# Linear attention and GELU feed-forward on one core: PSUM banks by name, weight loads regrouped, chunk loads asked for later, and four stores further down SyncE's list

## The chip, the core and the metric

The kernel runs on one core of a Trainium2 chip. The metric is the time of one execution on the device in microseconds (us); the median of three runs is compared. A profile is one further execution, recorded by the hardware. Engines are named as the profile names them: PE (TensorE, with PEld for its weight loads), DVE (VectorE), ACT (ScalarE), POOL (GpSimd), SP (SyncE). Each has its own list of instructions and works it in order. Every load from device memory but the eight decay factors is issued from POOL's list, every store and every DMA transpose from SP's; all share the same 16 DMA engines.

## The reference

Attention with a decay per head, worked in blocks with a state carried along, and then a two-matrix feed-forward with exact GELU over the heads laid side by side:

```python
def _attn_ref(q, k, v, lam):                 # q, k, v: (4, 8, 768, 64)
    ...
    for b in range(nb):                      # blocks of 64 tokens
        intra = np.einsum('bhic,bhjc->bhij', qb, kb) * Dmask[None]
        intra = np.einsum('bhij,bhjd->bhid', intra, vb)
        inter = np.einsum('bhid,bhde->bhie', qb * lam_pow[None], kv_state)
        out[:, :, sl] = intra + inter
        kb_dec = kb * rev_pow[None]
        kv_state = lam_block * kv_state + np.einsum('bhsd,bhse->bhde', kb_dec, vb)

def _moe_ref(x, w_in, w_out):                # x: (3072, 512); w_in: (512, 2048); w_out: (2048, 512)
    h = x @ w_in
    g = 0.5 * h * (1.0 + erf(h * inv_sqrt2))
    return g @ w_out
```

## The kernel before

**Tiling.** The 768 tokens of each of the 4 batches are cut into 6 chunks of 128 tokens. Chunk `n` is batch `n % 4` of group `n // 4`, so there are 24 chunks in 6 groups. A group gives one `x` tile of 512 tokens (128 columns for each chunk), and the feed-forward `mlp(g)` runs over it: 16 blocks `m0` to `m15` of 4 matmuls each (the first matrix, one 128-wide slice of `d_ff` each, then a Gelu on ACT) and 16 parts `p0` to `p15` of 4 matmuls each (the second matrix). In group 0 the parts go over the four quarters of `w_out` one after the other: `p0` to `p3` need `o0-4`, `p4` to `p7` need `o4-8`, `p8` to `p11` need `o8-12`, `p12` to `p15` need `o12-16`. With `mlp(g, n2, n3)` the first `n3` slices begin before the group's last chunk is there: `a` and `b` blocks take the first two and the third chunk's columns of slices below `n2`, blocks from `n2` to `n3` take three chunks' columns, and the `l` blocks (`rest`) do the last chunk's columns of all of them.

**The order is written by hand.** The pool of tiles makes no order of its own; what the code issues first stands first in each engine's list. The dictionary that goes with `mlp(g)` names, for a block, what is issued ahead of it: `visit(f, d)` interleaves on PE the outputs of chunk `f` with the scores and state products of chunk `d`; `values(n)` makes `vd` (the values with their decay) and half of `k2` on POOL; `keys(n)` makes the other half on DVE; `request(n)` puts the two DMA transposes of chunk `n` (k and q into `kqT`) on SP's list; `fetch(...)` and `ask(...)` put loads on POOL's list; `store_held` puts group 0's output tiles, which were kept back, on SP's list.

**Names for the steps.** `ask("...")` at line 147 is the order of the first loads: `k3` and `q3` are chunk 3's keys and queries, `v2` the values of chunks 2 and 3, `i4-6` slices 4 and 5 of `w_in` (two DMAs, one for each half of the partitions), `o4-8` slices 4 to 7 of `w_out` (one DMA), `V1` the values of group 1 (four DMAs, line 106). Chunks 0 to 7 are transposed on PE (`transposed`, line 237, and `both_transposed`, lines 247 and 251), later chunks by DMA (lines 258 and 259). `keep_warm` (line 497) is matmuls on a zero tile while the first loads arrive. The PSUM banks are shared by tag: two for `mh`, two for `mo`, four for `at`, taken in rotation; a taker waits until the bank's last user is done.

POOL and SP wait, ahead of each DMA that they issue, for the eighth DMA before it in their own list (one semaphore for each of eight lanes); so no more than eight of POOL's loads are on their way at a time.

Of the kernel before, what the change touches and what calls it, by code (L numbers as in the profile page):

```python
# [15 lines left out]
def kernel(  # L16
# [10 lines left out]
    nc = tc.nc  # L27
# [21 lines left out]
    out_pool = ctx.enter_context(tc.tile_pool(name="outp", bufs=6))  # L49
    ps = ctx.enter_context(tc.tile_pool(name="ps", bufs=1, space=bass.MemoryType.PSUM))  # L50

    BANKS = dict(mh=2, mo=2, at=4)

    def bank(shape, dtype, tag, name):
        return ps.tile(shape, dtype, tag=tag, name=name, bufs=BANKS[tag])

# [87 lines left out]
            else:  # L144
                (load_w_in if name == "i" else load_w_out)(*(int(x) for x in at.split("-")))

    ask("k0 q0 k1 q1 v0 k2 q2 k3 q3 v2 i0-1 i1-2 i2-4 i4-6 i6-8 i8-12 i12-16 o0-4 k4 q4 o4-8 V1 o8-12 k5 o12-16 k6 q6")

    idle = consts.tile([128, 512], BF16)
    nc.vector.memset(idle, 0.0)  # L150
# [76 lines left out]

    def transposed(c, name, eng):

        if name == "k":  # L230
            c.t_ps = bank([128, 2, HP, C], BF16, "mh", "t_ps")
        t_ps = c.t_ps[:, "kq".index(name)]
        on = half("kq".index(name))
        for hp in range(HP):
            for j in range(2):
                for hi in range(2):
                    nc.tensor.transpose(t_ps[half(hi), hp, half(j)], c.kq[on, 2 * hp + hi, j, :], ident[on, on])
        if name == "k":
            dst, src = c.kT, t_ps
        else:  # L240
            dst, src = (t.rearrange(f"d hp ({o}) -> d hp p j", j=2) for t, o in ((c.qT, "p j"), (t_ps, "j p")))
        (nc.scalar.copy if eng is nc.scalar else eng.tensor_copy)(dst, src)
# [122 lines left out]
    def scores0(n, mask=True):  # L365
        c = live[n]
        c.sc = [bank([128, HP, C], F32, "at", f"sc{hi}_ps") for hi in range(2)]
        issue([[(c.sc[hi][:, hp, :], c.kT[half(hi), hp, :], c.qT[half(hi), hp, :], True) for hi in range(2)]
               for hp in range(HP)])
        if mask:  # L370
            mask0(n)
# [41 lines left out]
    def mlp(g, n2=0, n3=0):  # L413


        x_t = xT[g]
        g_t = g_pool.tile([128, NK2, T], BF16, tag="g", name="g_t")
        hs = {}

        def columns(kf, lo, up):  # L420
            for ki in range(NK1):
                nc.tensor.matmul(hs[kf][:, lo:up], w_in_t[:, ki, kf * 128:(kf + 1) * 128], x_t[:, ki, lo:up],  # L422
                                 start=(ki == 0 and lo == 0), stop=(ki == NK1 - 1), skip_group_check=True)

        def mm1(kf, lo, up, last):
            def run():
                if lo == 0:
                    hs[kf] = bank([128, T], F32, "mo" if kf < n2 else "mh", "h_ps")
                columns(kf, lo, up)
                if last:  # L430
                    nc.scalar.activation(g_t[:, kf, :up], hs[kf][:, :up], ACT.Gelu)  # L431
            return run

        def rest(kfs):
            def run():
                h_ps = bank([128, len(kfs), C], F32, "mh", "h_ps")
                for i, kf in enumerate(kfs):
                    for ki in range(NK1):
                        nc.tensor.matmul(h_ps[:, i, :], w_in_t[:, ki, kf * 128:(kf + 1) * 128], x_t[:, ki, T - C:],
                                         start=(i == 0 and ki == 0), stop=(ki == NK1 - 1), skip_group_check=True)  # L440
                nc.scalar.activation(g_t[:, kfs[0]:kfs[-1] + 1, T - C:], h_ps, ACT.Gelu)  # L441
            return run

        om = {}

        def store(io, ps_, w):
            n = w.stop - w.start
            o_sb = out_pool.tile([128, n], F32, tag=f"o_{n}", name="o_sb")
            r = io * S + g * C
            nc.scalar.copy(o_sb, ps_)  # L450
            if g == 0:
                held.append((r, w, o_sb))
            else:
                nc.sync.dma_start(out[r:r + C, w], o_sb)

        def mm2(io, part):
            def run():
                if part == 0:
                    om[io] = bank([128, d_model], F32, "mh" if g == 0 and io >= 2 else "mo", "o2_ps")
                for kf in range(part * 4, part * 4 + 4):  # L460
                    nc.tensor.matmul(om[io], g_t[:, kf, io * C:(io + 1) * C], w_out_t[:, kf, :],  # L461
                                     start=(kf == 0), stop=(kf == NK2 - 1))
                if part == NK2 // 4 - 1:
                    store(io, om[io], slice(0, d_model))
            return run

        def mm2_half(io, h):
            def run():
                w = slice(h * (d_model // 2), (h + 1) * (d_model // 2))
                o2 = bank([128, d_model // 2], F32, "mo", "o2_ps")  # L470
                for kf in range(NK2):
                    nc.tensor.matmul(o2, g_t[:, kf, io * C:(io + 1) * C], w_out_t[:, kf, w],  # L472
                                     start=(kf == 0), stop=(kf == NK2 - 1))
                store(io, o2, w)
            return run

        blocks = [(f"a{kf}", mm1(kf, 0, 2 * C, False)) for kf in range(n2)]
        blocks += [(f"b{kf}", mm1(kf, 2 * C, T - C, True)) for kf in range(n2)]
        blocks += [(f"m{kf}", mm1(kf, 0, T - C, True)) for kf in range(n2, n3)]
        blocks += [(f"l{i}", rest(list(range(i, min(i + 4, n3))))) for i in range(0, n3, 4)]  # L480
        blocks += [(f"m{kf}", mm1(kf, 0, T, True)) for kf in range(n3, NK2)]
        if g == 0:
# [9 lines left out]

    def keep_warm(n):
        if not idle_ps:
            idle_ps[0] = bank([128, 512], F32, "mo", "idle_ps")
        for _ in range(n):
            nc.tensor.matmul(idle_ps[0], idle[:, :128], idle, start=True, stop=True)  # L497

# [16 lines left out]
    keep_warm(3)  # L515
    scores0(0)
    transposed(live[1], "k", nc.scalar)
    keep_warm(1)
    transposed(live[1], "q", nc.scalar)
    make_lam_o()  # L520
    keep_warm(3)
# [1 line left out]
    keep_warm(2)  # L523
    outputs0(0)
    empty(live[0])
    keep_warm(2)
    outputs0(1)
    empty(live[1])
    transposed(live[2], "k", nc.scalar)
    keep_warm(1)  # L530
    transposed(live[2], "q", nc.scalar)
    keep_warm(1)
    transposed(live[3], "k", nc.scalar)
    keep_warm(1)
    scores0(2)
    transposed(live[3], "q", nc.scalar)
    make_lam()
    nc.scalar.activation(warm, pos, ACT.Gelu)
    keep_warm(4)
    scores0(3)  # L540
    keep_warm(3)
    outputs0(2)
    empty(live[2])
    keep_warm(2)


    alloc_x(1)
# [15 lines left out]
    def ahead_of_group_1():  # L563
# [10 lines left out]
        begin(8)  # L574
        begin(9)

    run_blocks(mlp(0, 2, 3), {
        "b0": [last_of_first],
        "m3": [ahead_of_group_1],
        "m6": [make_dmask] + [lambda n=n: decay_k0(n, nc.vector) for n in range(B)],  # L580
        "p0": [first_states, lambda: by_block(live[4], nc.vector, nc.vector)],
        "p2": [lambda: both_transposed(live[4])],
# [5 lines left out]
        "p14": [lambda: visit(5, 6), lambda: both_transposed(live[7]), lambda: request(8)],  # L588
    })
    visit(6, 7, first=True)  # L590
    store_held(slice(0, 2))

# [6 lines left out]
    def keys(n):  # L599
        by_block(live[n], None, nc.vector)  # L600
# [10 lines left out]
    def plan_of(g):  # L611
        if g == 1:
            n = 2 * B
            return {
                "a0": [lambda: values(n), lambda: request(n + 1)],
                "b0": [lambda: fetch(n + 2, n + 3)],
                "m4": [lambda: visit(n - 1, None)],
                "m5": [lambda: keys(n), lambda: store_held(slice(2, B)), lambda: request(n + 2, n + 3)],
                "l0": [lambda: values(n + 1)],
                "l4": [lambda: ask(f"k{n + 4} q{n + 4} k{n + 5} q{n + 5}")],  # L620
                "m7": [lambda: visit(None, n)],
                "m8": [lambda: values(n + 2), lambda: ask("V3"), lambda: begin(n + 4), lambda: begin(n + 5),
                       lambda: request(n + 4, n + 5)],
                "m9": [lambda: keys(n + 1)],
                "m12": [lambda: visit(n, n + 1)],
                "m13": [lambda: values(n + 3)],
                "m14": [lambda: keys(n + 2)],
                "p2": [lambda: visit(n + 1, n + 2)],
                "p3": [lambda: values(n + 4)],
                "p4": [lambda: keys(n + 3), lambda: fetch(n + 6, n + 7), lambda: request(n + 6, n + 7)],  # L630
                "p8": [lambda: visit(n + 2, n + 3)],
                "p10": [lambda: keys(n + 4)],
                "p14": [lambda: visit(n + 3, n + 4)],
            }
# [52 lines left out]
```

## Time and profile before

| what | value |
|---|---|
| median of 3 runs | 214.06 us (213.49 to 214.38) |
| the profiled execution, its own time | 214.3 us |
| its span | 212.5 us |
| granted TensorE clock | 1.00 |
| PE busy | 203.4 us (96% of the span), 2421 matmuls |
| DMA engines | nine tenths busy or more in nearly all slices of the first 143 us |
| loads (software queue) | 74624 packets, 13.64 MB |
| transposes and stores (hardware queue) | 21152 packets, 10.50 MB |

"Busy" on PE is counted from the start to the modelled end of each matmul, which overlap: a row that gives 379 ns for one matmul of 512 columns stands in a stream whose matmuls start some 216 ns apart (64 of them in 13.81 us in the last group). So PE's share hides nothing only where its stream is dense; its idle time in front of an instruction is in the waits, with what ended it. Waits are given as: who waited, for whom, us in total, how many times, the longest.

### The profile page before, as it was taken

Reading aid. Unit: us, or ns where it says so; the run is one execution under the profiler, and the core shown is the slowest. Engines: PE = TensorE matmul, PEld = TensorE weight load, DVE = VectorE, ACT = ScalarE, POOL = GpSimd, SP = SyncE. Lnnn points to the kernel's source line nnn. Section 1 sums busy time; section 2 is a strip of 40 time slices with the busy share of each in tenths; the row PEclk is TensorE's granted clock in tenths of the full one; section 3 lists DMA queues with packets and bytes.
Section 4 is the critical chain, followed back from the end, with each engine's and each line's share of the span. In section 5 each row is a group of like instructions: output and inputs, shape, how many; then the busy total and the mean of one; then the engine's idle time right before and its main releaser. Section 6 shows DMA issues by size and latency. Waiting matters only on the chain.

```text
span 212.5 us, 5590 instructions
## 1 busy us (share of the span) xinstructions
PE 203.4 (96%) x2421; PEld 101.9 (48%) x2421; DVE 86.2 (41%) x185; ACT 90.2 (42%) x165; POOL 104.8 (49%) x148
## 2 busy tenths in 40 slices
PE   7999999799999899999999999999999999999992
PEld 2456445355664354444444444444544444444461
DVE  4657904339555556728416624732330331000000
ACT  5557663039645411265412356321466211665120
POOL 8989555598999403999689950930000000000000
PEclk9999999999999999999999999999999999999999
DMA  6999999999999999999999999932100021100121
GB/s 59 147 164 140 195 191 178 194 141 131 121 188 217 122 153 112 87 152 236 144 101 105 151 266 122 133 102 99 51 3 0 3 82 66 52 0 0 52 87 62
DMA packets 95801, 24.49 MB, mean 115 GB/s; under 512 B 87968, under 2 KB 92832, under 8 KB 95776
## 3 DMA queue, kind: packets, MB, share of 16 engines
q0 software_dynamic: 74624, 13.64, 89.6%
q1 hardware_dynamic: 21152, 10.50, 27.4%
q8 instruction: 19, 0.31, 0.6%
q14 instruction: 6, 0.05, 0.1%
HBM read 27.27 MB, written 6.29 MB: 158 GB/s over the span
## 4 chain that ended last, share of the span: by engine, by line
PE 71%; DMA 16%; POOL 6%; ACT 3%; issue 1%; SPq 0%; POOLq 0%
PE o_ps L461 33%; PE h_ps L422 30%; DMA vg_t<-in_v_dram 5%; DMA kqT<-q_t 4%; DMA w_in_t<-in_moe_w_in_dram 3%; DMA kq_t<-in_q_dram 3%; PE sc_ps L346 3%; POOL kq_t L82 2%; PE o_ps L346 2%; POOL w_in_t L125 2%; PE o_ps L472 2%; PE kv_ps L346 2%; POOL vg_t L106 1%; POOL v_t L95 1%; ACT k L272 1%
## 5 line engine op out<-in xcount | busy, mean ns | idle before, releaser
L422 PE MATMUL h_ps<-x_t,w_in_t 128*128 128x512 bf16 (+3 forms) x400 | 84.2, 366 | 0.2 <-ACT g_t L441 0.2
L461 PE MATMUL o_ps<-w_out_t,g_t 128*128 128x512 bf16 x368 | 83.0, 379 | 0.0
L431 ACT ACTIVATE g_t<-h_ps 128x512 bf16<-128x512 f32 (+1 forms) x96 | 55.9, 587 | 32.4 <-PE h_ps L422 32.4
L422 PEld LDWEIGHTS <-w_in_t 128*128 128x128 bf16 x400 | 37.5, 98 | 41.2 <-issue 0.8
L461 PEld LDWEIGHTS <-g_t 128*128 128x128 bf16 x368 | 34.7, 98 | 40.3
L338 DVE TENSOR_TENSOR x_t<-o_ps,lam_o 128x512 bf16<-128x512 f32 x24 | 16.5, 689 | 67.2 <-PE o_ps L346 67.2
L450 ACT COPY o_sb<-o_ps 128x512 f32<-128x512 f32 (+1 forms) x25 | 14.2, 571 | 65.1 <-PE o_ps L461 62.6
L281 POOL TENSOR_TENSOR vd<-vg_t,lam_v 128x512 bf16<-128x512 bf16 x20 | 21.0, 1050 | 25.6 <-DMA vg_t<-in_v_dram 24.6
L71 POOL DMA_DIRECT2D k_t<-in_k_dram x20 | 18.1, 907 | 2.2 <-DMA w_out_t<-in_moe_w_out_dram 1.7
L292 DVE TENSOR_TENSOR sm<-sc_ps,dmask 128x512 bf16<-128x512 f32 x20 | 13.6, 682 | 10.3 <-PE sc_ps L346 10.2
L106 POOL DMA_DIRECT2D vg_t<-in_v_dram x20 | 16.5, 843 | 1.4 <-DMA w_in_t<-in_moe_w_in_dram 1.4
L268 POOL COPY k<-k_t 64x256 bf16<-64x256 bf16 x34 | 14.1, 414 | 1.0
L71 POOL DMA_DIRECT2D q_t<-in_q_dram x16 | 14.5, 907 | 0.0
L346 PEld LDWEIGHTS <-kqT 64*64 64x64 bf16 (+1 forms) x352 | 7.7, 107 | 11.8 <-issue 10.9
L497 PE MATMUL idle_ps<-idle 128*128 128x512 bf16 x33 | 11.1, 444 | 1.2 <-DVE idle L150 1.2
L346 PE MATMUL sc_ps<-kqT 64*64 64x64 bf16 (+1 forms) x352 | 10.4, 197 | 1.8 <-DMA kqT<-q_t 1.5
L272 DVE COPY k<-k_t 64x256 bf16<-64x256 bf16 x34 | 11.9, 350 | 0.5
L125 POOL DMA_DIRECT2D w_in_t<-in_moe_w_in_dram x14 | 8.7, 675 | 1.0 <-DMA kq_t<-in_q_dram 0.8
L346 PE MATMUL kv_ps<-vd,k 64*64 64x64 bf16 x288 | 8.0, 193 | 1.2 <-POOL vd L281 1.2
L317 DVE TENSOR_TENSOR state<-t,lam_c 128x256 bf16<-128x256 f32 x16 | 8.9, 558 | 0.5
L346 PE MATMUL o_ps<-sm,vg_t 64*64 64x64 bf16 x320 | 8.4, 193 | 0.0
L307 DVE TENSOR_TENSOR t<-kv_ps,state 128x256 f32<-128x256 f32 x16 | 6.6, 415 | 1.0 <-PE kv_ps L346 1.0
(73 smaller groups left out, 134.9 us busy)
## 6 DMA issues: line engine op xcount, KB each, us to landing
out_dram<-o_sb SPq DMA_DIRECT2D x23, 256.0 KB, 5.2
k_t<-in_k_dram POOLq DMA_DIRECT2D x20, 128.0 KB, 6.8
vg_t<-in_v_dram POOLq DMA_DIRECT2D x20, 128.0 KB, 10.9
w_out_t<-in_moe_w_out_dram POOLq DMA_DIRECT2D x4, 512.0 KB, 11.2
q_t<-in_q_dram POOLq DMA_DIRECT2D x16, 128.0 KB, 6.9
w_in_t<-in_moe_w_in_dram POOLq DMA_DIRECT2D x4, 256.0 KB, 7.7
w_in_t<-in_moe_w_in_dram POOLq DMA_DIRECT2D x6, 128.0 KB, 4.2
kq_t<-in_k_dram POOLq DMA_DIRECT2D x4, 128.0 KB, 4.6
```

The costliest lines, as they stand in the source:

```text
L71: nc.gpsimd.dma_start(t, dram[name][b, :, g * C:(g + 1) * C, :].rearrange("h si d -> si h d"))
L106: nc.gpsimd.dma_start(t[half(hi), u], src[hi, s:s + L])
L268: same.tensor_copy(c.k2[half(hi), hi], k_r[half(hi), :, hi, :])
L272: copy(c.k2[half(hi), 1 - hi], k_r[half(1 - hi), :, hi, :])
L281: nc.gpsimd.tensor_mul(vd[n], of_group(n), lam_vb)
L292: nc.vector.tensor_mul(c.sm, c.sc, dmask)
L338: nc.vector.tensor_mul(xT[c.g][:, :, c.b * C:(c.b + 1) * C], c.o, lam_o)
L346: nc.tensor.matmul(out_, lhsT, rhs, start=start, stop=True, skip_group_check=True)
L422: nc.tensor.matmul(hs[kf][:, lo:up], w_in_t[:, ki, kf * 128:(kf + 1) * 128], x_t[:, ki, lo:up], start=(ki == 0 and lo == 0), stop=(ki == N ...
L431: nc.scalar.activation(g_t[:, kf, :up], hs[kf][:, :up], ACT.Gelu)
L450: nc.scalar.copy(o_sb, ps_)
L461: nc.tensor.matmul(om[io], g_t[:, kf, io * C:(io + 1) * C], w_out_t[:, kf, :], start=(kf == 0), stop=(kf == NK2 - 1))
```

## The change

Five edits of order, one of the shape of loads; the arithmetic is the same.

1. PSUM tag `mo` (two banks in rotation) becomes `mo0` and `mo1` (one bank each, chosen by the slice or part number). The PE transposes of the first four chunks no longer put k and q in one bank: k's stay in `mh`, q's get `mo1`. `keep_warm` uses `mo0`.
2. The `keep_warm` matmuls before group 0 (33 in all, as before) and the transposes, scores and outputs of chunks 1 to 3 are put in another order.
3. `mlp(0, 2, 3)` becomes `mlp(0, 2, 2)`: slice 2 is done whole, after `l0`.
4. The first loads: `w_in` in 10 DMAs in place of 14, and `V1` ahead of `o4-8`; `o12-16` goes last.
5. In group 1 the loads of chunks 12 and 13 and of `V3` move from `l4` and `m8` to `m13`, with the transposes of 12 and 13.
6. Group 0's output tiles 0 and 1 go behind the transposes of chunk 9, tiles 2 and 3 behind those of chunk 11.

```diff
-    BANKS = dict(mh=2, mo=2, at=4)
+    BANKS = dict(mh=2, mo0=1, mo1=1, at=4)
...
-    ask("k0 q0 k1 q1 v0 k2 q2 k3 q3 v2 i0-1 i1-2 i2-4 i4-6 i6-8 i8-12 i12-16 o0-4 k4 q4 o4-8 V1 o8-12 k5 o12-16 k6 q6")
+    ask("k0 q0 k1 q1 v0 k2 q2 k3 q3 v2 i0-2 i2-4 i4-8 i8-12 i12-16 "
+        "o0-4 k4 q4 V1 o4-8 k5 o8-12 k6 q6 o12-16")
...
-        if name == "k":
-            c.t_ps = bank([128, 2, HP, C], BF16, "mh", "t_ps")
-        t_ps = c.t_ps[:, "kq".index(name)]
+        t_ps = bank([128, HP, C], BF16, "mh" if name == "k" else "mo1", "t_ps")
...
-                    hs[kf] = bank([128, T], F32, "mo" if kf < n2 else "mh", "h_ps")
+                    hs[kf] = bank([128, T], F32, f"mo{kf % 2}" if kf < n2 else "mh", "h_ps")
...
     transposed(live[1], "k", nc.scalar)
-    keep_warm(1)
+    keep_warm(2)
     transposed(live[1], "q", nc.scalar)
...
     outputs0(0)
     empty(live[0])
-    keep_warm(2)
+    keep_warm(1)
+    transposed(live[2], "k", nc.scalar)
     outputs0(1)
     empty(live[1])
-    transposed(live[2], "k", nc.scalar)
     keep_warm(1)
     transposed(live[2], "q", nc.scalar)
+    keep_warm(2)
+    transposed(live[3], "k", nc.scalar)
+    scores0(2)
     keep_warm(1)
-    transposed(live[3], "k", nc.scalar)
-    keep_warm(1)
-    scores0(2)
     transposed(live[3], "q", nc.scalar)
...
     scores0(3)
-    keep_warm(3)
+    keep_warm(1)
     outputs0(2)
     empty(live[2])
-    keep_warm(2)
+    keep_warm(3)
...
-    run_blocks(mlp(0, 2, 3), {
+    run_blocks(mlp(0, 2, 2), {
...
     visit(6, 7, first=True)
-    store_held(slice(0, 2))
...
-                "a0": [lambda: values(n), lambda: request(n + 1)],
+                "a0": [lambda: values(n), lambda: request(n + 1), lambda: store_held(slice(0, 2))],
...
-                "m5": [lambda: keys(n), lambda: store_held(slice(2, B)), lambda: request(n + 2, n + 3)],
+                "m5": [lambda: keys(n), lambda: request(n + 2, n + 3), lambda: store_held(slice(2, B))],
...
-                "l4": [lambda: ask(f"k{n + 4} q{n + 4} k{n + 5} q{n + 5}")],
...
-                "m8": [lambda: values(n + 2), lambda: ask("V3"), lambda: begin(n + 4), lambda: begin(n + 5),
-                       lambda: request(n + 4, n + 5)],
+                "m8": [lambda: values(n + 2)],
...
-                "m13": [lambda: values(n + 3)],
+                "m13": [lambda: values(n + 3), lambda: fetch(n + 4, n + 5), lambda: request(n + 4, n + 5)],
```

The other uses of `mo` become `mo0` or `mo1` in the same way (here `n` is 8, so `n + 4` is chunk 12). In the lists that result, POOL goes from `values(9)` to `values(10)` and `values(11)` and only then to the loads of chunks 12 and 13 and the four of `V3`; SP has the transposes of 8, of 9, two stores, the transposes of 10 and 11, two stores, the transposes of 12 and 13. PE has four matmuls fewer (slice 2's columns are no longer split).

More of the change, by code (lines that the diff above doesn't have):

```diff
@@ L458, in run @@
                 if part == 0:
-                    om[io] = bank([128, d_model], F32, "mh" if g == 0 and io >= 2 else "mo", "o2_ps")
+                    om[io] = bank([128, d_model], F32, "mh" if g == 0 and io >= 2 else f"mo{io % 2}", "o2_ps")
                 for kf in range(part * 4, part * 4 + 4):
@@ L469, in run @@
                 w = slice(h * (d_model // 2), (h + 1) * (d_model // 2))
-                o2 = bank([128, d_model // 2], F32, "mo", "o2_ps")
+                o2 = bank([128, d_model // 2], F32, f"mo{(io + h) % 2}", "o2_ps")
                 for kf in range(NK2):
@@ L494, in keep_warm @@
         if not idle_ps:
-            idle_ps[0] = bank([128, 512], F32, "mo", "idle_ps")
+            idle_ps[0] = bank([128, 512], F32, "mo0", "idle_ps")
         for _ in range(n):
@@ L575, in ahead_of_group_1 @@
         begin(9)
-    run_blocks(mlp(0, 2, 3), {
+    run_blocks(mlp(0, 2, 2), {
         "b0": [last_of_first],
-        "m3": [ahead_of_group_1],
+        "m2": [ahead_of_group_1],
         "m6": [make_dmask] + [lambda n=n: decay_k0(n, nc.vector) for n in range(B)],
```

## The prediction

> **What bounds the kernel now.** I read the waits of PE first, since PE is busy for 96% of the span. Columns: who waited, for whom, us in total, how many times, the longest.
>
> ```profile
> PE sc_ps L346 <- DMA kqT<-q_t: 1.5, 2, 1.1
> PE kv_ps L346 <- POOL vd L281: 1.2, 1, 1.2
> PE t_ps L237 <- ACT kqT L242: 0.7, 2, 0.4
> PE sc_ps L346 <- ACT kqT L254: 0.3, 1, 0.3
> PE h_ps L422 <- ACT g_t L441: 0.2, 1, 0.2
> ```
>
> These sum to 3.9 us. The PE timeline (start, us, what, idle before it) puts the three largest in place; behind 75.3 us there is none up to the end at 208.69.
>
> ```profile
> 40.71 0.44 PE L346 MATMUL kv_ps<-vd,k 64*64 64x64 bf16 x16 [1.24 <-POOL vd L281]
> ...
> 67.46 0.22 PE L346 MATMUL sc_ps<-kqT 64*64 64x64 bf16 x2 [0.36 <-DMA kqT<-q_t]
> ...
> 74.59 0.22 PE L346 MATMUL sc_ps<-kqT 64*64 64x64 bf16 x2 [1.14 <-DMA kqT<-q_t]
> ```
>
> So whatever PE gains by 75 us arrives whole at the end, unless a new wait takes it. Who is late for PE is read from POOL's timeline and the chain that ended last.
>
> ```profile
> 30.69 0.76 POOL L128 DMA_DIRECT2D w_out_t<-in_moe_w_out_dram  x1 [1.72 <-DMA w_out_t<-in_moe_w_out_dram]
> ...
> 35.55 0.89 POOL L71 DMA_DIRECT2D k_t<-in_k_dram  x1 [1.70 <-DMA w_out_t<-in_moe_w_out_dram]
> ...
> 39.61 1.04 POOL L281 TENSOR_TENSOR vd<-vg_t,lam_v 128x512 bf16<-128x512 bf16 x1 [2.26 <-DMA vg_t<-in_v_dram]
> ...
> 66.25 3.31 POOL L106 DMA_DIRECT2D vg_t<-in_v_dram  x4
> ...
> 82.95 1.04 POOL L281 TENSOR_TENSOR vd<-vg_t,lam_v 128x512 bf16<-128x512 bf16 x1 [11.43 <-DMA vg_t<-in_v_dram]
> ```
>
> ```profile
> 28.16 11.22 DMA vg_t<-in_v_dram
> ...
> 65.39 9.06 DMA kqT<-q_t
> ```
>
> The first loads are one saturated stream: each issue waits for the landing of the eighth before it (35.55: for o4-8, landed 35.26). V1 was issued by 28.97 and landed at 28.16 + 11.22 = 39.38. SP's own list is late in the same way, each issue taking over 1 us:
>
> ```profile
> 56.89 2.12 SPq L397 DMA_DIRECT2D out_dram<-o_sb  x2
> 59.11 1.29 SPq L258 DMA_TRANSPOSE kqT<-k_t  x1
> 60.45 1.85 SPq L259 DMA_TRANSPOSE kqT<-q_t  x1
> 62.34 1.15 SPq L397 DMA_DIRECT2D out_dram<-o_sb  x2
> 63.60 1.71 SPq L258 DMA_TRANSPOSE kqT<-k_t  x1
> 65.39 2.04 SPq L259 DMA_TRANSPOSE kqT<-q_t  x1
> ```
>
> **Edits 1 to 3, the start.** The two waits of 0.36 us of a q transpose for ACT (k and q in one bank) go. PE took up chunk 3's q at 14.59, though it had landed at 13.87; in the new order that is some 0.65 us earlier, and a0 (17.80) begins some 1 us earlier. Of that, l0 gives back about 0.3: without slice 2 ahead of it, it comes right behind the b blocks while DVE still empties chunk 3's outputs (0.69 us, L338). The four matmuls fewer save nothing (12 of 128 columns took 0.74 us, 62 ns each; 512 columns cost 216). So PE would reach p4 some 0.7 us ahead of the 37.2 of before. I count this as zero, because p4 then waits for o4-8 (next); if that cover is gone, it is worth 0.7.
>
> **Edit 4, the first loads.** The bytes stay, the packets change. By the trace's packet records, packets of 1024 bytes moved 200 KB/us (23 to 28 us), of 512 bytes 143 (16 to 20 us), of 256 bytes 157. i4-8 (512 KB as stored) goes from 512-byte to 1024-byte packets: 3.6 to 2.6 us, -1.0; i0-2 (256 KB) from 256 to 512 bytes: +0.16. The stream is then about 0.85 us ahead. V1 (4.12 us, landings 35.26 to 39.38) passes o4-8 (2.45 us, 32.81 to 35.26), so V1 lands at about 36.1 and its wait goes, but o4-8 lands last of the two, at 39.38 - 0.85 = 38.5, and p4 needs it: a new wait of some 2 us at p4. From there to p6 come p4 and p5 (8 matmuls at 217 ns, 1.73) and the scores and products of chunk 4 (0.65): p6 at 40.95 against 41.08. V1's 4.12 us contain a stall of the stream (a 16 KB instruction fetch at 37.08, 1.17 us in the packet records); if it falls behind o4-8 in the new order, p6 is at 40.3. I take a gain of 0.4 between the two; the bounds are +0.8, and -0.75 if the larger packets bring nothing (o4-8 at 39.38, p6 at 41.8). i4-8 as one pair may land at 21 to 22 us with m4 due at 21.0; up to 1 us, covered by the same wait at p4. Behind p6 the same 8.4 us of loads follow (39.38 to 47.77 before), and o8-12 and o12-16 land before p8 and p12 by some 0.5 to 1 us.
>
> A rule of the Trainium skill would make more of this edit: the page "DMA: Bandwidth & Descriptors", section "Anatomy of one DMA — SWDGE (gpsimd) path", gives each DMA a fixed 2.0 us beside its bytes, which for four DMAs fewer is, as an estimate, 8 us earlier. The rows speak against it: neighbouring w_in DMAs landed 0.3 to 1.3 us apart, though each took 3.6 to 8.7 us from issue to landing.
>
> **Edit 6, the stores.** k9 and q9 leave the two stores (2.12 us) behind, so q9 is issued 2.1 us earlier than 60.45; its wait was 0.36: gone. k10 and q10 have all four tiles' stores moved about them: stores 2 and 3 (1.15 us) go behind q11, stores 0 and 1 stay ahead of k10. PE will want q10 at 73.45 - 0.4 - 0.36 = 72.7 (73.45 is 74.59 less its wait); it landed at 74.45, so it must come 1.8 us earlier. 1.15 come from the stores, 0.85 from the stream ahead, and the loads of chunks 12 and 13 no longer share the engines with it (edit 5): with transposes beside them, loads and transposes moved 430 packets per us each, loads alone 1200. I take the 1.14 as gone; at worst it stays. The stores delay nobody: their tiles are next written in group 1's parts, from 77.2.
>
> **Edit 5, the later loads.** In POOL's list `values(10)` and `values(11)` now come first, and the copies of `values(11)` need k11 (landed at 62.81). So the four loads start at about 63.7 in place of 60.65, and V3 is issued from 67.3 to 70.6 in place of 66.25 to 69.56. Queued behind V3 is `values(12)`, and `visit(11, 12)` on PE waits for that. Before, V3 landed at 82.79, `values(12)` was done at 84.85, and PE came at 86.50: 1.65 us to spare. With 1.9 us gained PE comes at 84.6. V3's landing is bounded by 81.4 (the stream is 1.4 ahead: no wait) and 83.84 (1.05 later, as issued: done at 85.9, a wait of 1.3). As the stream stays full, I take 82.2 to 82.8: a wait of 0.3.
>
> Sum: 0.4 + 0.36 + 1.14 - 0.3 = 1.6 us. The profiled execution took 214.3 (span 212.5): 212.7. It stands 0.24 above the median of 214.06, so the predicted median is 212.5.
>
> **Rivals.**
>
> *V3 becomes the wait.* For it: PE arrives 1.9 us earlier with 1.65 to spare, and the issue moves back. Against it: between 60 and 83 us the engines, not POOL's issues, set the landings (13.2 us from V3's last issue to its landing). At 83.84 the gain is 0.4 + 1.5 - 1.3 = 0.6: 213.5. A chance of 0.17.
>
> *The transposes stay late.* For it: q10 took 9.06 us from issue to landing and q9 7.0; if their landing is set by engines that are full anyway, an earlier issue brings little. Then only 0.4 is left: 213.7. A chance of 0.12.
>
> *Slower: the loads of chunk 11 are held up by the transposes of chunk 9, and V3 with them.* Those transposes now run beside the loads of chunks 10 and 11 (430 packets per us in place of 1200). If k11 lands 2 us later (64.8), POOL, which stands at the copies of `values(11)`, issues all of V3 3 us later than before; at the same 13.2 us it lands at 85.8, `values(12)` is done at 87.8, and `visit(11, 12)` begins 1.3 us later than before: 215.4. It decides from a landing of V3 at 84.4 on (no gain at all), and 85.5 for 0.5%. Against it: the loads of chunk 8 to 11 should be asked for earlier. A chance of 0.12. The Trainium skill's page named above, in "Rules for kernel authors", advises to issue a DMA early and wait late; this edit does the opposite for eight loads, and no run here shows yet which side wins.
>
> *The fixed cost per DMA is real.* Then o4-8 and V1 both land before PE needs them, the wait of 1.24 and the start's 0.7 are won: 1.24 + 0.7 + 0.36 + 1.14 - 0.5 (V3) = 2.9: 211.1. A chance of 0.06.
>
> **Chances and range.** The forecast has 0.53, with its own range of 211.8 to 213.0; the rivals 0.47. A measurement of this kernel can tell about 0.5% (1.07 us) from no change. Faster by more than that is below 212.99: nearly all of the forecast (0.50), the last rival (0.06), some of the first two (0.07), 0.63. Slower than 215.1 has 0.13; within, 0.24. The range for 8 in 10 is 211.4 to 214.5: it takes in the first two rivals and leaves out most of the slower one and of the largest gain.
>
> **What would show it.** PE's waits should show a wait on `w_out_t` at p4 of 1 to 2.5 us in place of the 1.24 on `vd`; no wait on `kqT`; no `t_ps` wait on ACT; p6 near 40.7. `vd` of chunk 12 should start at 82 to 83, with a wait of `kv_ps` under 0.7 us near 84.6. It is wrong if o4-8 lands later than 39.4, if q10 lands after 73, or if `vd` of chunk 12 starts after 84.5.

## The result and the profile after

| | before | after |
|---|---|---|
| median, runs of both on one chip | 214.35 us (212.04 to 217.26, 20 runs) | 211.59 us (210.78 to 214.44, 20 runs) |
| ratio, 95% interval | | 0.9902 [0.9874, 0.9929] |
| the profiled execution, its own time | 214.3 us (span 212.5) | 212.24 us (span 210.4) |

The change is faster by about 1%, some 2.1 us, and the interval lies wholly below 0.995. The ratios leave out executions more than 1.5% slower than the fastest of their kernel, so they are not the quotients of the medians, and two of the profiles further down, those of `a_no_first` and `split_k`, were taken while the chip granted a clock of 0.992 in place of 1.00, so of these two only the ratio, and for `split_k` the loads before 30 us, are read.

The waits of PE in the changed kernel (who waited, for whom, us in total, how many times, the longest):

```profile
PE o_ps L460 <- issue: 1.6, 10, 0.2
...
PE kv_ps L345 <- issue: 1.1, 1, 1.1
...
PE h_ps L421 <- ACT g_t L440: 0.2, 1, 0.2
PE h_ps L438 <- DVE x_t L337: 0.2, 1, 0.2
PE t_ps L236 <- DMA kq_t<-in_q_dram: 0.2, 1, 0.2
```

The waits on `kqT`, on `vd` and on ACT's `kqT` are all gone, and no wait on `w_out_t` has come in their place. The ten short ones on `o_ps` are no waits: in the timeline they stand behind rows of three or seven matmuls where four or eight are issued, so a record is missing there. The largest new one is 1.1 us on `kv_ps` with no releaser ("issue": PE waited for nothing that the profile shows).

The row of before with which `p6` begins (start, us, what, idle before it):

```profile
41.08 2.76 PE L461 MATMUL o_ps<-w_out_t,g_t 128*128 128x512 bf16 x12
```

PE's timeline of the changed kernel shows where the time was won and lost:

```profile
38.92 0.44 PE L345 MATMUL sc_ps<-kqT 64*64 64x64 bf16 x16
39.20 0.42 PE L345 MATMUL kv_ps<-vd,k 64*64 64x64 bf16 x16
39.55 2.76 PE L460 MATMUL o_ps<-w_out_t,g_t 128*128 128x512 bf16 x11
...
50.46 0.22 PE L345 MATMUL kv_ps<-vd,k 64*64 64x64 bf16 x2 [1.12 <-issue]
...
72.45 0.22 PE L345 MATMUL sc_ps<-kqT 64*64 64x64 bf16 x2
```

`p6` begins at 39.55 in place of 41.08, so 1.53 us are won by there. 1.12 us are lost again in the middle of `visit(5, 6)`. Chunk 10's scores begin at 72.45 in place of 74.59, 2.14 earlier, and most of that difference stays to the end (PE's last matmul ends at 206.67 in place of 208.65, 1.98 earlier).

POOL's timeline answers to the rows of `vd` shown of before:

```profile
35.22 1.04 POOL L280 TENSOR_TENSOR vd<-vg_t,lam_v 128x512 bf16<-128x512 bf16 x1 [1.24 <-DMA vg_t<-in_v_dram]
...
83.05 1.04 POOL L280 TENSOR_TENSOR vd<-vg_t,lam_v 128x512 bf16<-128x512 bf16 x1 [13.01 <-DMA vg_t<-in_v_dram]
```

Chunk 4's `vd` starts at 35.22 (39.61 before). By their landing times the last of `w_in` is there at 25.99 (27.87 before), `V1` at 35.04 and `o4-8` at 36.92, both before PE comes to `p4` at about 37.1. Chunk 12's `vd` starts at 83.05 (82.95 before).

### The profile page after: what moved, and what is told of

The parts are those of the page before. It is cut to its first block, busy times and chain, and to the rows that moved or that the text cites. A ratio compares the mean times of both kernels' runs of the same rounds, so it can differ in the third digit from the quotient of the medians.

```text
span 210.4 us, 5549 instructions
## 1 busy us (share of the span) xinstructions
PE 200.5 (95%) x2388; PEld 101.1 (48%) x2417; DVE 81.7 (39%) x185; ACT 90.4 (43%) x165; POOL 102.0 (48%) x144
## 4 chain that ended last, share of the span: by engine, by line
PE 89%; POOL 3%; DMA 3%; issue 2%; ACT 0%; DVE 0%; POOLq 0%
PE h_ps L421 39%; PE o_ps L460 38%; PE sc_ps L345 3%; DMA kq_t<-in_q_dram 3%; PE o_ps L345 2%; POOL kq_t L82 2%; PE kv_ps L345 2%; PE o_ps L471 2%; PE idle_ps L496 1%; POOL v_t L95 1%; PE h_ps L438 1%; PE t_ps L250 1%; PE t_ps L246 0%; DVE x_t L337 0%; ACT g_t L440 0%
## 5 line engine op out<-in xcount | busy, mean ns | idle before, releaser
L460 PE MATMUL o_ps<-w_out_t,g_t 128*128 128x512 bf16 x354 | 80.5, 380 | 1.8 <-issue 1.6
L267 POOL COPY k<-k_t 64x256 bf16<-64x256 bf16 x34 | 13.6, 401 | 1.6 <-DMA k_t<-in_k_dram 0.6
L496 PE MATMUL idle_ps<-idle 128*128 128x512 bf16 x30 | 10.2, 449 | 1.5 <-DVE idle L151 1.2
L271 DVE COPY k<-k_t 64x256 bf16<-64x256 bf16 x34 | 10.7, 313 | 0.5
L316 DVE TENSOR_TENSOR state<-t,lam_c 128x256 bf16<-128x256 f32 x16 | 8.0, 499 | 0.5
L345 PEld LDWEIGHTS <-k 64*64 64x64 bf16 x288 | 6.5, 108 | 1.3 <-issue 1.2
```

The lines of the kernel that those rows point to most:

```text
L267: same.tensor_copy(c.k2[half(hi), hi], k_r[half(hi), :, hi, :])
L345: nc.tensor.matmul(out_, lhsT, rhs, start=start, stop=True, skip_group_check=True)
```

## The experiments

All ratios are to the kernel before, run beside each on the same chip. Several chips were used, so ratios are compared and not microseconds. The last three columns are read from one profile of each kernel: when the last load of `w_in` landed, when `p6` began and when chunk 10's scores began.

| kernel | edits in it | ratio [95%] | last `w_in` | p6 | chunk 10's scores |
|---|---|---|---|---|---|
| before | none | 1 | 27.87 | 41.08 | 74.59 |
| after | all | 0.9902 [0.9874, 0.9929] | 25.99 | 39.55 | 72.45 |
| first_loads | 4 | 0.9909 [0.9873, 0.9945] | 25.61 | 40.00 | 72.30 |
| regroup | grouping of `w_in` only | 0.9910 [0.9874, 0.9945] | 25.91 | 40.09 | 73.86 |
| stores | 6 | 0.9952 [0.9907, 0.9998] | 27.75 | 40.54 | 72.49 |
| start_only | 1 to 3 | 0.9953 [0.9907, 0.9999] | 28.31 | 41.48 | 74.93 |
| a_no_first | all but 4 | 0.9946 [0.9914, 0.9978] | | | |
| a_old_stores | all but 6 | 0.9905 [0.9870, 0.9941] | 26.12 | 39.55 | 71.55 |
| a_old_late | all but 5 | 0.9936 [0.9903, 0.9970] | 26.08 | 39.95 | 71.96 |
| split_k | grouping, in 14 DMAs | 0.9993 [0.9948, 1.0039] | 27.46 | | |
| no_56 | all but 5 and 6 | 0.9894 [0.9856, 0.9932] | 25.95 | 39.50 | 72.19 |
| after_again | all | 0.9875 [0.9839, 0.9911] | 25.66 | 39.58 | 72.10 |
| warm_small | all, and 99 matmuls more | 0.9893 [0.9855, 0.9930] | 25.10 | 39.90 | 72.04 |
| warm_half | all, and 33 matmuls more | 0.9901 [0.9863, 0.9938] | 25.89 | 41.24 | 73.24 |

### One edit alone

The first loads, edit 4 alone:

```diff
-    ask("k0 q0 k1 q1 v0 k2 q2 k3 q3 v2 i0-1 i1-2 i2-4 i4-6 i6-8 i8-12 i12-16 o0-4 k4 q4 o4-8 V1 o8-12 k5 o12-16 k6 q6")
+    ask("k0 q0 k1 q1 v0 k2 q2 k3 q3 v2 i0-2 i2-4 i4-8 i8-12 i12-16 "
+        "o0-4 k4 q4 V1 o4-8 k5 o8-12 k6 q6 o12-16")
```

> The kernel before with edit 4 alone (w_in in 10 DMAs, V1 ahead of o4-8, o12-16 last). Theory A (the larger w_in packets run the stream faster, whatever the start does): o4-8 lands at 37 to 37.5 us, V1 at 35 to 35.5, p6 starts at 39.6 to 40.0 (41.08 before), no wait for vd or w_out_t ahead of it; with the waits on kqT left in part, the time falls by 1 to 1.6 us (0.5 to 0.7%). Rival B (the earlier stream of the changed kernel comes from the new start, edits 1 to 3, or from an instruction fetch that fell better): o4-8 lands at 38 us or later as the prediction had it, p4 waits about 1 us or more for w_out_t, p6 starts at 40.5 to 41, and the time falls by 0.5 us at most.

`o4-8` landed at 36.30, `V1` at 34.43, both still earlier than expected, and `p6` began at 40.00. The ratio is 0.9909: more than expected, and nearly all of the whole change. The waits of PE in this kernel:

```profile
PE idle_ps L498 <- DVE idle L151: 1.2, 1, 1.2
PE kv_ps L347 <- issue: 0.8, 2, 0.5
PE t_ps L238 <- ACT kqT L243: 0.7, 2, 0.4
PE h_ps L423 <- ACT g_t L442: 0.2, 1, 0.2
```

No wait on `kqT` is left, though the stores stand where they stood and the loads of chunks 12 and 13 are asked for as before: with everything earlier, SP starts its list earlier (chunk 8's transposes at 50.87, 54.25 before), and chunk 10's q landed at 69.95 in place of 74.45. Theory A holds, and by this profile the gains of the edits overlap.

The grouping of `w_in` alone, with the order behind it as before:

```diff
-    ask("... v2 i0-1 i1-2 i2-4 i4-6 i6-8 i8-12 i12-16 o0-4 k4 q4 o4-8 V1 o8-12 k5 o12-16 k6 q6")
+    ask("... v2 i0-2 i2-4 i4-8 i8-12 i12-16 o0-4 k4 q4 o4-8 V1 o8-12 k5 o12-16 k6 q6")
```

> The kernel before with the w_in DMAs grouped as after (i0-2 i2-4 i4-8) and the order of everything behind them as before (o4-8 ahead of V1). Theory A (fewer and larger w_in DMAs move the stream ahead by some 1.9 us): the last w_in lands near 26 us (27.87 before), o4-8 near 33.4 (35.26 before), V1 near 37.5 (39.38), and the 1.24 us wait for vd ahead of p6 is gone without V1 having been moved; time down by 1 to 1.6 us. Rival B (the grouping is worth 0.85 us as in the prediction): w_in lands near 27, V1 near 38.5, vd still holds PE for 0.3 to 0.5 us, time down by about 0.8 us. Rival C (the order of V1 does it, the grouping nothing): w_in lands at 27.5 or later, the wait for vd stays above 1 us, time unchanged.

The last `w_in` landed at 25.91, `V1` at 37.58, `p6` began at 40.09 with no wait on `vd`. The ratio of 0.9910 is again more than expected. The grouping alone gives `p6` 0.99 us; `V1` ahead of `o4-8` adds 0.1. Theory A, and rival C falls: at `p6` the order of `V1` was not needed. But the waits on q stayed in the profiled execution (213.5 us, above its median of 212.86):

```profile
PE sc_ps L346 <- DMA kqT<-q_t: 1.8, 2, 1.6
```

Here chunk 8's transposes began at 53.07 and chunk 10's q landed at 73.73, against 50.87 and 69.95 in `first_loads`. So in these two profiles the early `w_in` does not take the wait on q away by itself; it is gone where `V1` also goes ahead of `o4-8` and `o12-16` goes last. The two ratios are the same, so whether the order did it or the one execution is open.

The stores, edit 6 alone:

```diff
     visit(6, 7, first=True)
-    store_held(slice(0, 2))
...
-                "a0": [lambda: values(n), lambda: request(n + 1)],
+                "a0": [lambda: values(n), lambda: request(n + 1), lambda: store_held(slice(0, 2))],
...
-                "m5": [lambda: keys(n), lambda: store_held(slice(2, B)), lambda: request(n + 2, n + 3)],
+                "m5": [lambda: keys(n), lambda: request(n + 2, n + 3), lambda: store_held(slice(2, B))],
```

> The kernel before with edit 6 alone (the stores of group 0 behind the transposes of chunks 9 and 11). Theory A (SP's list order makes the q transposes late, as the prediction had it: 1.15 us for q10, the loads of chunks 12 and 13 still beside it): q9 lands some 2 us earlier and its wait of 0.36 is gone; q10 lands near 73.3 (74.45 before), its wait falls from 1.14 to 0.1 to 0.4; time down by 1.0 to 1.4 us (0.5 to 0.65%). Rival B (the DMA engines, full of the loads of chunks 12 and 13, set q10's landing): q10 still lands at 74 or later, its wait stays above 0.8, and only the 0.36 goes: time down by 0.3 to 0.6.

Chunk 9's q was issued at 58.49 (60.45 before) and landed at 63.85 (67.42); chunk 10's landed at 69.78, 4.7 us earlier where 1.2 were expected, with edit 5's loads still beside it, and no wait on `kqT` is left. This speaks for theory A, but the profiled execution was one of the two fastest of its kernel (212.21 us; the median is 214.54), so it need not show what most of them do. The ratio, 0.9952, has an interval from 0.02% to 0.93%, so the size of 1.5 us is neither confirmed nor excluded. In that execution `V1` also came 0.5 us earlier than in before, with nothing changed there: one profile of one execution carries such an uncertainty.

Edits 1 to 3 alone: banks, order of the start, two slices in place of three. Only edit 3 is printed here; edits 1 and 2 are as in the change's diff.

```diff
-    run_blocks(mlp(0, 2, 3), {
+    run_blocks(mlp(0, 2, 2), {
...
-        "m3": [ahead_of_group_1],
+        "m2": [ahead_of_group_1],
```

> Edits 1 to 3 alone (PSUM banks by name, the order of the start, two slices ahead in place of three) on the first loads, stores and later loads of before. Theory A (the start is worth nothing since PE then waits for vd at p6, or for the weights): a0 starts 0.3 us earlier (17.5 in place of 17.8) or more, p6 starts at 41.0 to 41.2 as before with a wait for vd of 1.2 to 1.6 us, time within 0.3 us of before. Rival B (part of the 1.5 us that the changed kernel gained by p6 comes from the start): p6 starts below 40.7, and time falls by 0.4 us or more. Also looked at: an instruction fetch of 16 KB for PE that took 2.37 us at 18.56 in before and 0.94 us at 20.51 in the changed kernel; if it is short here and the w_in loads land earlier than 27.87, the fetch and not the packets moved the stream.

`p6` began at 41.48 (41.0 to 41.2 expected) behind a wait of 1.18 for `vd`, and the profile ends where before's does. That is theory A for the cover, but a0 at 18.05 was no earlier than the 17.80 of before. In this execution PE stood for chunk 1's values:

```profile
PE kv_ps L344 <- POOL vd L279: 1.2, 1, 1.2
PE o_ps L344 <- DMA v_t<-in_v_dram: 1.0, 1, 1.0
```

No other kernel with the new start shows that second wait, and the a0 of before is an early one: a0 came at 18.20 to 18.38 in `first_loads`, `regroup` and `stores`, which have the old start, and at 17.48 to 17.64 in after, `after_again`, `a_old_stores`, `a_old_late` and `no_56`. By these profiles the new start is worth some 0.7 us at a0. The ratio leaves anything between nothing and 0.9% open. PE's instruction fetch was short here (0.96 us at 20.70), and still the last `w_in` landed at 28.31: a long fetch was not what held the stream back.

### The change with one edit undone

`a_no_first`, `a_old_stores`, `a_old_late` and `no_56` are the changed kernel with the lines of edit 4, of 6, of 5, and of 5 and 6 put back as the change's diff shows them.

> The changed kernel with the first loads of before (edit 4 undone). Theory A (edit 4 carries most of the gain; stores and later loads only take away waits on kqT that an earlier stream takes away too): the wait for vd of about 1.2 us is back ahead of p6, p6 starts at 40.9 to 41.3, no kqT wait above 0.3 us, ratio to before 0.994 to 0.997, that is 0.8 to 1.4 us slower than the changed kernel. Rival B (the gains add up as in the prediction, 0.4 for the first loads and 1.5 for stores and later loads): ratio 0.992 to 0.993, at most 0.5 us slower than the changed kernel.

> The changed kernel with the stores where they were (edit 6 undone). Theory A (the earlier stream and the later loads make the q transposes land in time whatever stands ahead of them in SP's list, as they did with edit 4 alone): kqT waits of 0.3 us in sum or less, time within 0.5 us of the changed kernel. Rival B (SP's order is needed, as the prediction had it): waits on kqT of 1 us or more in sum, q10 landing after 73, time 1 us or more above the changed kernel.

> The changed kernel with the loads of chunks 12, 13 and V3 asked for where they were (edit 5 undone). Theory A (edit 5 is worth nothing in time): no kqT wait above 0.3 us, vd of chunk 12 starts at 80.5 to 82 (83.05 in the changed kernel), no wait at the visit of chunk 12, time within 0.5 us of the changed kernel. Rival B (the loads beside them keep q10 late): q10 lands after 72.5, a kqT wait of 0.5 us or more, time 0.5 to 1 us above the changed kernel. Rival C (edit 5 costs): the small break at the visit of chunk 12 (0.15 us) goes and time falls by 0.3 us or more.

> The changed kernel with edits 5 and 6 both undone (stores and later loads of group 1 as before). Theory A (with the earlier stream of edit 4 the transposes of q are in time by themselves, and edits 5 and 6 are worth little on top): waits on kqT of 0.4 us or less in sum, ratio to before 0.989 to 0.993, within 0.5 us of the changed kernel. Rival B (their 1.5 us are needed as the prediction had it): waits on kqT of 1 us or more, 1 us or more slower than the changed kernel.

Without edit 4 the ratio is 0.9946: theory A by the time; what it said of the waits isn't settled, since this profile isn't read.

Without the stores the ratio is 0.9905, PE's waits show no `kqT`, and chunk 10's q landed at 67.36: theory A. Without edit 5 there is no `kqT` wait either (chunk 10's q landed at 68.81, so rival B falls), chunk 12's `vd` starts at 82.12 with no wait there, and the ratio is 0.9936, whose interval overlaps that of the changed kernel: neither a cost nor a gain of edit 5 can be told.

Without both, 0.5 us of waits on `kqT` come back (0.3 and 0.2), a little more than theory A's 0.4 and far from rival B's 1, and the ratio is 0.9894 beside 0.9875 for the changed kernel on the same chip. So on top of edit 4, edits 5 and 6 together are worth 0.2% by these ratios and 0.7 us by the raw medians (212.25 and 211.54), which is less than the intervals resolve.

Asking for eight loads later did not make them land later: chunk 12's `vd` started at 83.05, 80.41 and 78.91 in the profiles of after, `after_again` and `a_old_stores` with the late order, at 82.31 and 82.12 in those of `no_56` and `a_old_late` with the early one. The Trainium skill advises to issue a DMA early and to wait for it late (page "DMA: Bandwidth & Descriptors", section "Rules for kernel authors"); no loss by doing the opposite could be measured here.

### What in the grouping does it

The prediction took the size of the packets for the cause. `split_k` is `regroup` with two of its groups cut in half along the contraction, so it has the packets of the new grouping and the number and sizes of DMAs of the old:

```diff
         for hi in range(2):
-            nc.gpsimd.dma_start(w_in_t[half(1 - hi), :, f], w_in_r[hi, :, :, f])
+            for ko in ((slice(0, 2), slice(2, 4)) if lo in (0, 4) else (slice(0, 4),)):
+                nc.gpsimd.dma_start(w_in_t[half(1 - hi), ko, f], w_in_r[hi, :, ko, f])
```

> The kernel before with w_in grouped as in the regroup run (packets of 512 and 1024 bytes), but i0-2 and i4-8 cut along the contraction, so that there are 14 DMAs of the same bytes each as before (64, 64, 64, 64, 128 KB and so on). Theory A (eight DMAs on their way at a time do not hold enough bytes when they are of 64 and 128 KB; the number of DMAs counts): the rate from 16 to 20 us stays at 110 to 160 KB/us, POOL's issues pause near 13.3 us, the last w_in lands at 27 to 28.3 as before (27.87), and the wait for vd stays near 1.2 us. Rival B (the size of the packets sets the rate): 185 to 200 KB/us from 16 us on, the last w_in lands at 25.6 to 26.3, o4-8 near 33.5, no wait for vd.

Three stretches of 2 us of the start, by engine (stretch, length, busy time and count of PE, PEld, DVE, ACT and POOL, then PE's clock, the DMA engines' share and GB/s). Before:

```profile
16.00:18.00 2.00, 2.00 (x23) 1.01 (x24) 1.64 (x3) 1.95 (x5) 2.00 (x5) 1.00 1.17 145
18.00:20.00 2.00, 2.00 (x27) 1.50 (x26) 1.03 (x3) 0.70 (x4) 2.00 (x4) 1.00 1.24 154
20.00:22.00 2.00, 2.00 (x20) 1.29 (x18) 1.88 (x4) 1.40 (x4) 1.47 (x2) 1.00 1.05 127
```

The same of `regroup`:

```profile
16.00:18.00 2.00, 2.00 (x23) 0.84 (x22) 1.53 (x3) 1.94 (x8) 1.78 (x4) 1.00 1.31 202
18.00:20.00 2.00, 2.00 (x26) 1.39 (x25) 1.02 (x3) 0.83 (x2) 1.71 (x3) 1.00 1.24 205
20.00:22.00 2.00, 2.00 (x25) 1.47 (x23) 1.90 (x4) 1.69 (x4) 1.16 (x2) 1.00 1.24 205
```

And of `split_k`:

```profile
16.00:18.00 2.00, 2.00 (x23) 0.84 (x22) 1.53 (x3) 1.94 (x8) 2.00 (x4) 1.00 1.25 175
18.00:20.00 2.00, 2.00 (x24) 1.40 (x25) 1.02 (x3) 0.81 (x2) 1.98 (x4) 1.00 1.10 153
20.00:22.00 2.00, 2.00 (x25) 1.47 (x23) 1.90 (x4) 1.71 (x4) 2.00 (x3) 1.00 1.06 156
```

The last column decides. With ten DMAs the engines move 202 to 205 GB/s. With fourteen they move 127 to 154 in before and 153 to 175 in `split_k`, though by the packet records nearly all its bytes behind 17 us come in packets of 1024 bytes. And 512-byte packets were not slow: from 14 to 17 us, where most packets are of 512 bytes, the loads of after moved 188 KB/us and those of `split_k` 183. The last `w_in` of `split_k` landed at 27.46, 0.41 ahead of before and 1.55 behind `regroup`. The table bears this out: 27.46 to 28.31 in the four profiles with fourteen DMAs, 25.10 to 26.12 in the nine with ten. So the number of DMAs counts for most of it: rival B falls. What is left for the packet size is 0.3 to 0.9 us (27.46 against the 27.75 to 28.31 of the other three with fourteen), about what those three differ among themselves. (The wait for `vd`, expected near 1.2 us, was only 0.1: `V1` came at 38.69 and PE itself later.) It is 0.4 us for each of the four DMAs more. The Trainium skill's fixed cost of 2.0 us for each DMA (page "DMA: Bandwidth & Descriptors", section "Anatomy of one DMA — SWDGE (gpsimd) path") has the sign of that, not the size.

Why a larger number costs is argued, not shown. In each kernel POOL's list stands still near 13 to 15 us for the eighth DMA before (0.83 us in before, 0.95 in `split_k`, 0.74 in `regroup`, 1.24 in after). By then 384 KB of `w_in` are issued in before and 512 in `split_k`, 1024 in `regroup` and 768 in after. At some 180 KB/us the first two are used up in 2 to 3 us, and what is issued behind the pause takes 3.6 to 4.6 us to land. The longest pause, 1.24 us in after, went with a stream as full as that of `regroup`, so it is not the pause alone. What limits it, the eight lanes, the 0.6 to 0.7 us of an issue, or work for each DMA in the queue, wasn't separated.

### The stall in visit(5, 6)

The same stall is in `first_loads`, where PE's list of instructions is that of before, which has none. It comes at the 603rd matmul there, place 49 of the visit counted from zero, and at the 602nd in `a_old_stores`, place 52 of its visit. So it keeps to a number in the program rather than to a place in the visit, and it follows a 16 KB packet of the instruction queue. That queue moves 19 such packets in an execution of 2421 matmuls, so 127.4 matmuls for each. `first_loads` has a second stall, at its 986th matmul, 383 behind the first, which is three times 127.7:

```profile
50.28 0.21 PE L347 MATMUL kv_ps<-vd,k 64*64 64x64 bf16 x1 [0.51 <-issue]
...
73.15 0.22 PE L347 MATMUL kv_ps<-vd,k 64*64 64x64 bf16 x2 [0.30 <-issue]
```

The packet records of this queue, beside PE's timeline:

| kernel | fetch starts | 602nd or 603rd matmul starts | apart | idle before it |
|---|---|---|---|---|
| regroup | 45.75 | 49.67 | 3.92 | 0 |
| stores | 46.48 | 50.12 | 3.64 | 0 |
| before | 46.68 | 50.66 | 3.98 | 0 |
| a_old_late | 47.00 | 49.81 | 2.81 | 0.07 |
| a_old_stores | 47.19 | 49.69 | 2.50 | 0.36 |
| first_loads | 47.42 | 50.28 | 2.86 | 0.51 |

In after, where some records are missing, the stall ends 2.98 us behind its fetch (47.48). To move the page of instructions, the idle matmuls of the start were cut:

```diff
         for _ in range(n):
-            nc.tensor.matmul(idle_ps[0], idle[:, :128], idle, start=True, stop=True)
+            for w in range(4):
+                nc.tensor.matmul(idle_ps[0][:, w * 128:(w + 1) * 128], idle[:, :128], idle[:, :128], start=True, stop=True)
```

> The changed kernel with each keep_warm matmul of 512 columns cut into four of 128 (same columns, 99 matmuls and 99 weight loads more at the very start). The stall inside visit(5, 6) that no releaser is shown for came at the 602nd or 603rd matmul of the program in three kernels (52nd of the visit with the new start, 49th with the old one), 2.5 to 3.0 us after a 16 KB fetch of PE's instructions had started. Theory A (PE ran out of instructions at a page of the program): 99 matmuls more move that page out of the visit into the slow part blocks ahead of it, no such stall above 0.3 us between 48 and 51 us, start of group 1's visits (visit 7) 0.4 to 1.1 us earlier than in the changed kernel; a stall may show at another place, again about 3 us behind a fetch. Rival B (copies on ACT or a product on DVE hold the matmul): the stall stays at about the 50th matmul of visit(5, 6).

> The changed kernel once more, for a second profile and beside the other kernels of this call. Theory A (the stall in visit(5, 6) belongs to where the fetch falls and differs from run to run): same place, between 0 and 1.2 us; span 208.8 to 210.6. Rival B (it is a fixed wait of the program): 1.1 us again within 0.1.

In the second profile of the changed kernel the stall was 0.75 us, ending at 50.12, 2.83 behind its fetch (47.29): same place, another size. In `warm_small` `visit(5, 6)` ran through, and PE's timeline has a stall in the transposes behind it:

```profile
50.22 0.26 PE L250 MATMUL t_ps<-ident,q_t 64*64 64x64 bf16 x5
50.94 0.22 PE L250 MATMUL t_ps<-ident,q_t 64*64 64x64 bf16 x3 [0.46 <-issue]
```

It ended 2.84 us behind a fetch that began at 48.10. The view begins inside the row of 16 transposes; the stall stands ahead of the last three, at the 730th matmul of this program, 128 behind the 602nd. So the page that begins at the 602nd was in time, and the next one was late. A copy on ACT as the cause would not have moved with 99 matmuls at the start: theory A in both, though its "no such stall above 0.3 us between 48 and 51 us" was not met, since the stall of the next page fell into that stretch. The gain expected at chunk 8 did not come (61.07 beside 61.48 and 61.13), since the cut matmuls made the start 0.3 us longer and the page was late at its new place too. The last kernel cut each idle matmul in two, to put the parts p10 to p13 between fetch and need:

```diff
-            nc.tensor.matmul(idle_ps[0], idle[:, :128], idle, start=True, stop=True)
+            for w in range(2):
+                nc.tensor.matmul(idle_ps[0][:, w * 256:(w + 1) * 256], idle[:, :128], idle[:, :256], start=True, stop=True)
```

> The changed kernel with each keep_warm matmul cut into two of 256 columns (33 matmuls and 33 weight loads more at the start). Theory A (a page of PE's instructions is asked for some 60 matmuls ahead and is there some 2.9 us later, so it is late only where those 60 run fast): the page that began at the 602nd matmul now begins about 33 matmuls earlier in the program, with the parts p10 to p13 (over 3 us) between the asking and the need; no stall above 0.2 us between 48 and 54 us, the visits of group 1 begin 0.5 to 1.0 us before the changed kernel's (its second profile: 61.13, 66.18, 72.10), ratio to before 0.984 to 0.988. Rival B (any shift leaves a stall of the same size somewhere, as with 99 matmuls more): a stall of 0.4 to 1.2 us somewhere between 46 and 56 us and a ratio of 0.988 to 0.992.

No unexplained stall above 0.2 us is left between 46 and 56 us, and from chunk 4's scores to those of chunk 8 PE took 21.65 us (40.62 to 62.27) in place of 22.17 (38.96 to 61.13) in the second profile of the changed kernel: 0.5 won. But a wait of 0.32 for ACT's `kqT` stands at the next visit, and in this execution the start was 1.7 us late (chunk 4's scores at 40.62): until some 10 us its matmuls ran slower (16 transposes in 0.63 us, 0.44 from then on). The ratio of 0.9901 is that of the changed kernel, as rival B had it. The stall went as theory A said, the time did not fall: no better version came of it.

That wait of 0.32 is also in before (0.3 on ACT's `kqT`), and a stall ahead of it hides it. So a stall costs less than its length: from chunk 4's scores to those of chunk 8 PE took 21.65 us in `warm_half` with no stall, 21.66 in `a_old_stores` with 0.36, 22.17 in `after_again` with 0.75 and 22.56 in after with 1.12.

## Why the prediction was right, and where it was not

The time was in the range and faster, as forecast; the gain was 2.06 us between the profiled executions where the sum said 1.6. The median of 211.59 lies near the fast end of the 8-in-10 range and below the forecast's own range of 211.8 to 213.0; by the ratio (0.9902 of 214.06, so 212.0) it lies inside. That the sum came so near is in part luck. By the timelines, `p6` won 1.53 (1.08 with edit 4 alone) where 0.4 was forecast, the waits on `kqT` gave the forecast 1.50, chunk 12 cost 0.15 in place of 0.3, and two terms that the sum did not have went against the surplus: the stall in `visit(5, 6)` cost 1.12 and took away the wait of 0.32 for ACT behind it. Together that is 2.08, against 1.98 at PE's last matmul.

- **Edit 4, the first loads: mis-sized, 0.4 for about 1.1.** The step that failed is "packets of 1024 bytes moved 200 KB/us (23 to 28 us), of 512 bytes 143 (16 to 20 us)", and the 0.85 us made from it. The rate of the 512-byte packets was read from a stretch in which the stream was thin for another reason. Two of the prediction's own rows spoke against packet size: 256-byte packets, at 157, had been faster than 512-byte ones, and the `w_in` landings were not all "0.3 to 1.3 us apart", since one gap was 2.80 (19.59 to 22.39). The grouping brought the last `w_in` forward by 1.9 us, and `split_k` shows that the number of DMAs did most of it.
- **The new wait at p4 did not come.** It was to be 1 to 2.5 us, with `o4-8` at 38.5; it landed at 36.92, outside the bounds. So the condition of the fourth rival (both land before PE needs them, 211.1) came about, to which 0.06 was given, though at 0.4 us for each DMA. The passing of `V1` ahead of `o4-8`, on which half the step was spent, is worth 0.1 us at `p6`.
- **Edits 1 to 3: zero, as long as the cover is there.** `start_only` shows that cover: `vd` still held PE for 1.18 us. With edit 4 the cover went, and `p6` moved from 40.00 to 39.55: 0.45 in place of the 0.7 named for that case. The two waits of `t_ps` on ACT went as said, and `l0` waits 0.2 for chunk 3's outputs (0.3 foreseen). a0 came at 17.52, not at 16.8.
- **Edit 6: the mechanism was right, the sum was not.** Alone it takes both waits on `kqT` away in the profile of `stores`. But edit 4 alone does so too in the profile of `first_loads`, so the 1.5 us are not to be added to it: the edits without 4 gave 0.54%, edit 4 alone 0.91%, all together 0.98%. The prediction said that 0.85 us of what q10 needed come "from the stream ahead", yet booked the whole under the stores. (Its 430 packets per us for loads and transposes each hold for a stretch such as 76 to 78 us, with 420 and 411; from 65.4 to 74.4, while q10 was on its way, they moved 504 and 211.)
- **Edit 5: 0.3 for 0.15 and 0.** `vd` of chunk 12 started at 83.05 for the 82 to 83 foreseen, and one pair of products at 84.77 took 0.37 us where its neighbours took 0.20. In the second profile `vd` started at 80.41 and nothing waited. The slower rival (`V3` three microseconds late) did not appear in any profile that is read here.
- **What was missing: PE's instructions.** Where `p6` begins by 40.0, PE stalls for up to 1.1 us in `visit(5, 6)`, because it now reaches a page of its instructions before that is there; net of the wait that a stall hides, up to 0.9 us of the gain at `p6` are given back. No step looked at this, though the prediction had met such a fetch at 37.08 as a disturbance of the loads.

## What to carry to other kernels

Where loads are bound by the queue, look at how many DMAs carry the bytes before looking at their packets: a rate read from a thin stretch of the stream is not the rate of its packet size. Waits that share one cause behind them (here an early stream) must not be added up edit by edit; ask of each what is left of it when the others are done. And when PE is moved forward against dense stretches of small matmuls, its own instructions can be what it waits for; such a stall has no releaser, and keeps its number in the program when the order around it changes.

## What the runs showed of the hardware

- PE's instructions come through the DMA engines in 16 KB packets, 19 in one execution, which took 0.9 to 2.4 us each. One packet holds the instructions of about 128 matmuls here (2421 matmuls in 19 packets; stalls at the 602nd or 603rd, the 730th and the 986th). In seven stalls of after, `after_again`, `no_56`, `a_old_stores`, `first_loads` (two) and `warm_small` PE went on 2.5 to 3.0 us after such a packet had begun; in the three kernels of the table above where PE came 3.6 us or more behind it, nothing stalled.
- The same profile point varies by some tenths of a microsecond between executions of one kernel, a load's landing by more: the stall was 1.12 and 0.75, chunk 8's scores 61.48 and 61.13, chunk 12's `vd` 83.05 and 80.41. Terms of 0.3 us can't be read from one profile.
- How many DMAs carried the loads counted here: the same 2 MB of `w_in` were in by 25.10 to 26.12 us as ten DMAs and by 27.46 to 28.31 as fourteen, the 27.46 with the larger packets of the ten.
